# Decode attention: output weights of a group loaded in three transfers of unequal row counts instead of one, and bias sums issued earlier

## Chip, cores, metric

One core of a Trainium2 chip (trn2). The metric is device time of one execution in microseconds (us), taken on the chip. A run counts as slow here when it is over 1.5% above the fastest run of the same kernel. The profile is one execution recorded by the hardware profiler.

PE is the matrix engine, DVE the vector engine, SP the engine that issues the large loads here. SBUF is the on-chip memory of 128 partitions into which the loads write. The profile counts 16 DMA engines. A load comes in packets, and each K and V load here has 16 landings: a landing is taken as the moment at which one engine reports its share of a load done.

## The reference, cut to what matters

One token attends to a cache of 65,536 keys and values, with 16 query heads on 8 key/value heads of 256 numbers; a small MLP and a gate are mixed in.

```python
q = (x @ wq) as 16 heads
scores = q . k / 16        # k: 8 heads x 65536 x 256, bf16
o = softmax(scores) . v    # v: the same size
a = o @ wo                 # wo: 4096 x 448
out = g * a + (1 - g) * b  # b: the MLP; g: one sigmoid of the token
```

K and V are 537 MB together. `wo` is 3.7 MB, eight groups of 512 rows. The time is that of reading K and V: the queue of the large loads, 544.22 MB, is busy for 99.7% of it.

## The kernel before

The K and V cache comes in 48 steps of five or six blocks, each step one transfer of K and one of V over all 128 partitions (40,960 or 49,152 B a partition; only the last V comes in four pieces). SP issues all large loads on one queue. Two K buffers and one V buffer keep the queue full. DVE transposes K, PE makes scores and sums.

The output weights of groups 0 to 6 were one transfer each, behind V loads in the same queue:

```python
def load_wo(g):
    if g >= 1:
        sp.wait_ge(s_oo, g)                       # the last group's weights are used
    sp.dma_start(
        out=wo[:].rearrange("p r c n -> p r (c n)"),            # 128 partitions, 2 x 1792 B each
        in_=A_wo[g * 512:(g + 1) * 512, :].rearrange("(r p c) n -> p r (c n)", r=2, c=2),
    ).then_inc(s_wo, 16)
...
take(dve, s_wo, 16)                               # before the heads of that group are used
```

The end of the program, cut:

```python
pe.wait_ge(s_last[1], 16); upright(edges[1], edges[2])   # V . p, second piece of the last V block
drain_pv(False)                                          # DVE
row = acc + bias                                         # DVE
o_turn(2)                                                # PE, head turn (L685)
pe.wait_ge(s_last[2], 16); turned(edges[2], edges[3])    # PE, turned V blocks (L751)
pe.wait_ge(s_last[3], 16); turned(edges[3], edges[4])
heads()                                                  # DVE, oT (L550)
pe.wait_ge(s_fd, 2)
for a in range(4): matmul(acc4, one_f, row)              # PE, bias sums (L789)
for k in range(4): ... matmul(acc4, oT, wo)              # PE, output matmuls (L799), wait for s_wl[r]
```

The softmax here doesn't subtract the row's maximum and nothing guards it: scores larger than these inputs give would overflow.

## Time and profile before

| | before |
|---|---|
| time, median of 3 | 1265.88 us (1265.81 to 1265.99) |
| bytes read | 544.22 MB, 431 GB/s over the span |
| DMA queue of the large loads | 99.7% of the 16 engines' time |
| PE, DVE busy | 57%, 53% |
| 40,960 B packet, 49,152 B packet | 1514 ns, 1815 ns (8047 of 8064 and 4086 of 4096 packets) |
| 1792 B packet (output weights) | 74 ns (2039 of 2048 packets) |

The first fence is the page's slice view of the kernel before: the span in 40 equal slices, in the DMA line the busy share in tenths, in the next line the rate; then the packets, and the line of the one large queue.

```profile
DMA  9999999999999999999999999999999999999998
GB/s 407 425 435 429 442 435 424 439 433 432 440 430 426 436 434 437 440 426 434 438 427 438 430 436 436 430 432 436 430 443 429 429 439 434 429 442 430 430 436 348
DMA packets 16840, 544.30 MB, mean 431 GB/s; under 512 B 1856, under 2 KB 3906, under 8 KB 4162
...
q1 hardware_dynamic: 16744, 544.22, 99.7%
```

The rate lies at 424 to 443 GB/s between the start and the last slice. The kernel is bound by this stream.

The next fence is the view of stretches, 232 to 248 us, in which the output weights of group 1 come in (columns: stretch, its length, busy time of each engine, granted PE clock, DMA busy share, GB/s).

```profile
232.00:248.00 16.00, 9.17 (x77) 3.52 (x74) 5.91 (x4) 1.33 (x3) 1.69 (x2) 1.00 1.01 435
```

The last one is the chain of work that ended last (start us, duration us, what).

```profile
...
1228.07 30.50 DMA kbuf<-in_A_v_cache_dram
1258.57 0.05 issue
1258.62 1.44 PE misc L751 x48
1260.06 0.48 PE acc L789 x8
1260.54 0.50 PE acc L799 x16
1261.04 0.02 issue
1261.06 0.27 DVE res L806
```

It goes through the third piece of the last V block, then the turned blocks, the bias sums, the output matmuls. The trace's landings (one for each DMA engine of a transfer) show that 15 engines have this piece by 1257.75 us and one by 1258.57 us. The same spread, 1.7 us from first to last with one engine 0.8 us behind the fifteenth, stands in nearly every K and V load (93 of 95 lie between 1.6 and 1.85 us).

### The profile page before, as it was taken

What the parts mean: (1) busy time and instruction counts of PE and PEld (TensorE: products, weight loads), DVE (VectorE), ACT (ScalarE), POOL (GpSimd) and SP (SyncE); (2) the same over time, 40 slices, a digit from 0 to 9 for tenths busy, and PEclk for the clock granted to TensorE, in tenths of its full rate; (3) what the DMA queues carried; (4) which work ended last, traced back from release to release, by engine and by line L of the source; (5) the groups of instructions that cost most, each with busy time, mean ns of one, the idle gap of its engine ahead of it and who ended that gap; (6) DMA issues with size and microseconds to landing.
All of it is one profiled execution on the core that took longest, in us unless ns stands there. A gap on an engine that the chain in (4) does not pass through costs nothing. (4 is left out here: it accounts for less than half of the span.)

```text
span 1264.1 us, 10623 instructions
## 1 busy us (share of the span) xinstructions
PE 722.2 (57%) x4296; PEld 276.3 (22%) x4296; DVE 675.3 (53%) x462; ACT 50.1 (4%) x127; POOL 78.5 (6%) x111
## 2 busy tenths in 40 slices
PE   3855656456554665556654564555645656466556
PEld 1311222122221222112221221222212222122212
DVE  5745554465544555455555555464545645465544
ACT  0000000000000000000000000000000000000000
POOL 1001010110110101101011011000000000000000
PEclk9887777878787787777878787777877778778887
DMA  9999999999999999999999999999999999999998
GB/s 407 425 435 429 442 435 424 439 433 432 440 430 426 436 434 437 440 426 434 438 427 438 430 436 436 430 432 436 430 443 429 429 439 434 429 442 430 430 436 348
DMA packets 16840, 544.30 MB, mean 431 GB/s; under 512 B 1856, under 2 KB 3906, under 8 KB 4162
## 3 DMA queue, kind: packets, MB, share of 16 engines
q1 hardware_dynamic: 16744, 544.22, 99.7%
q8 instruction: 2, 0.03, 0.0%
q10 hardware_dynamic: 90, 0.01, 0.0%
q14 instruction: 4, 0.03, 0.0%
HBM read 544.22 MB, written 0.00 MB: 431 GB/s over the span
## 5 line engine op out<-in xcount | busy, mean ns | idle before, releaser
L661 PE MATMUL sc<-kT,qw 128*128 128x512 bf16 x2048 | 573.5, 438 | 482.9 <-PEq L657 482.9
L532 DVE STREAM_TRANSPOSE kT<-kbuf 128x2048 f32<-128x2048 f32 x256 | 572.8, 2285 | 330.1 <-DVEq L524 330.1
L661 PEld LDWEIGHTS sc<-kT,qw 128*128 128x128 bf16 x2048 | 211.1, 108 | 845.1 <-issue 692.8
L675 PE MATMUL pv<-vbuf,pT 128*4 128x512 bf16 x2008 | 121.2, 390 | 28.8 <-PEq L705 28.7
L543 DVE TENSOR_TENSOR og<-pv,og 128x512 f32<-128x512 f32 x40 | 27.7, 692 | 98.5 <-DVEq L524 97.9
L608 ACT ACTIVATE p_t<-sc 128x512 bf16<-128x512 f32 x48 | 28.7, 597 | 1191.9 <-PE sc L661 1191.9
L675 PEld LDWEIGHTS pv<-vbuf,pT 128*4 128x4 bf16 x2008 | 47.1, 88 | 99.3 <-issue 53.8
L589 DVE STREAM_TRANSPOSE pT<-p_t 128x512 bf16<-128x512 bf16 x32 | 22.8, 712 | 74.1 <-DVEq L524 74.1
L635 POOL TENSOR_SCALAR t_b<-t_b 128x448 f32<-128x448 f32 x14 | 7.9, 564 | 359.1 <-ACT t_b L617 359.1
L639 POOL TENSOR_SCALAR t_b<-t_b,hw 128x448 f32<-128x448 f32 x14 | 8.9, 638 | 334.0 <-ACT t_b L625 334.0
L579 DVE STREAM_TRANSPOSE pT<-p_t 128x512 bf16<-128x512 bf16 x8 | 5.7, 712 | 26.9 <-DVEq L524 26.9
L720 PE MATMUL acc<-wo,oT 128*1 128x448 bf16 x28 | 10.1, 504 | 12.7 <-PEq L717 12.7
L644 POOL TENSOR_TENSOR ymix<-ymix,t_b 128x448 f32<-128x448 f32 x14 | 16.1, 1148 | 1.1
L638 POOL TENSOR_TENSOR t_b<-t_b,u_b 128x448 f32<-128x448 f32 x14 | 15.8, 1127 | 1.2
L643 POOL TENSOR_TENSOR t_b<-t_b,u_b 128x448 f32<-128x448 f32 x14 | 15.8, 1126 | 1.2
L542 DVE COPY og<-pv 128x512 f32<-128x512 f32 x8 | 5.5, 692 | 18.9 <-DVEq L524 18.9
L594 DVE STREAM_TRANSPOSE pT<-p_t 128x512 bf16<-128x512 bf16 x8 | 5.7, 712 | 14.9 <-DVEq L524 14.9
L617 ACT ACTIVATE t_b<-h_bc,b1T,w1T 128x448 f32<-128x448 f32 x14 | 10.5, 748 | 0.0
L631 POOL TENSOR_SCALAR u_b<-h_bc,w1T,b1T 128x448 f32<-128x448 f32 x14 | 10.0, 715 | 4.1 <-DVE hw L428 2.7
L608 ACT ACTIVATION_READ_ACCUMULATOR p_t<-sc 128x1 f32 x48 | 9.3, 194 | 0.0
L685 PEld LDWEIGHTS misc<-mask,og 128*128 128x128 f32 x64 | 8.7, 196 | 2.4 <-DVE og L543 1.3
L477 DVE TENSOR_TENSOR qw<-qr,block 128x32 bf16<-128x32 f32 (+1 forms) x18 | 8.6, 561 | 0.1
(86 smaller groups left out, 77.4 us busy)
## 6 DMA issues: line engine op xcount, KB each, us to landing
kbuf<-in_A_k_cache_dram SPq DMA_DIRECT2D x32, 5120.0 KB, 33.2
vbuf<-in_A_v_cache_dram SPq DMA_DIRECT2D x31, 5120.0 KB, 20.4
kbuf<-in_A_k_cache_dram SPq DMA_DIRECT2D x16, 6144.0 KB, 35.7
vbuf<-in_A_v_cache_dram SPq DMA_DIRECT2D x16, 6144.0 KB, 23.5
wo<-in_A_wo_dram SPq DMA_DIRECT2D x7, 448.0 KB, 23.6
vbuf<-in_A_wq_dram SPq DMA_DIRECT2D x1, 3072.0 KB, 10.3
kbuf<-in_A_v_cache_dram SPq DMA_DIRECT2D x1, 2560.0 KB, 26.0
kbuf<-in_A_v_cache_dram SPq DMA_DIRECT2D x1, 1280.0 KB, 30.5
```

The costliest lines, as they stand in the source:

```text
L532: dve.transpose(out=kT[b][:].bitcast(FP32), in_=kn[:, s * SB * 128:(s + 1) * SB * 128]).then_inc(s_kt, 1)
L543: return dve.tensor_tensor(out=og[:], in0=pv[:], in1=og[:], op=ALU.add)
L589: dve.transpose(out=pT[:], in_=p_t[:]).then_inc(s_pt, 1)
L608: ins = act.activation(out=p_t[:], in_=sc[:], func=ACT.Exp, scale=scale, accum_out=den[:, c:c + 1])
L617: ins = act.activation(out=t_b[:], in_=h_bc[:], func=ACT.Square, scale=w1T[:, b:b + 1], bias=b1T[:, b:b + 1],)
L631: lambda: pool.tensor_scalar(out=u_b[:], in0=h_bc[:], scalar1=w1T[:, b:b + 1], scalar2=b1T[:, b:b + 1], op0=ALU.mult, op1=ALU.add,),
L638: lambda: pool.tensor_tensor(out=t_b[:], in0=t_b[:], in1=u_b[:], op=ALU.mult),
L643: lambda: pool.tensor_tensor(out=t_b[:], in0=t_b[:], in1=u_b[:], op=ALU.mult),
L644: lambda: pool.tensor_tensor(out=ymix[:], in0=ymix[:], in1=t_b[:], op=ALU.add),
L661: ins = pe.matmul(sc[:], lhsT=qw[:, q, at:at + 128], rhs=kv[:, :, q // 2, :, q % 2], start=(first and q == 0), stop=(last and q == 7), ski ...
L675: ins = pe.matmul(pv[32 * a:32 * a + 4, :], lhsT=pT[:, k, :, ROW0 + s], rhs=vt[:, j * DH:(j + 2) * DH], start=first and k < 4, stop=last a ...
L720: ins = pe.matmul(acc[0:1, 0:D], lhsT=oT[:, k:k + 1], rhs=wo[:, r, cc, :], start=False, stop=False, skip_group_check=True,)
```

## The change

The intent, as far as the diff shows it: give some DMA engines more rows of the output weights and others fewer, so that the engines finish together (the author's reading), and take the bias sums out of the end.

```diff
+SHARES = (
+    (96, 16, 16), (112, 11, 5), (112, 9, 7), (112, 13, 3), (112, 10, 6), (112, 12, 4), (112, 14, 2),
+)
@@
-            sp.dma_start(
-                out=wo[:].rearrange("p r c n -> p r (c n)"),
-                in_=A_wo[g * 512:(g + 1) * 512, :].rearrange("(r p c) n -> p r (c n)", r=2, c=2),
-            ).then_inc(s_wo, 16)
+            rows = A_wo[g * 512:(g + 1) * 512, :].rearrange("(r p c) n -> p r (c n)", r=2, c=2)
+            lo = 0
+            for n in SHARES[g]:
+                sp.dma_start(
+                    out=wo[lo:lo + n].rearrange("p r c n -> p r (c n)"), in_=rows[lo:lo + n]
+                ).then_inc(s_wo, 16)
+                lo += n
@@
-                        take(dve, s_wo, 16)
+                        take(dve, s_wo, 48)
@@
         o_turn(2)
+        pe.wait_ge(s_fd, 2)
+        for a in range(4):
+            pe.matmul(... one_f, row ...)          # bias sums, cut
         pe.wait_ge(s_last[2], 16)
         turned(edges[2], edges[3])
         ...
-        pe.wait_ge(s_fd, 2)
-        for a in range(4):
-            pe.matmul(... one_f, row ...)          # bias sums, cut
```

On how many engines a transfer of few rows runs, the traces show in counts, if each landing is one engine's. The three 14-row loads of before have 14 landings each. The seven loads of output weights have 16 each in before; in after they have 48 in group 0 (96, 16 and 16 rows) and 32 in each of groups 1 to 6, as 16 + 11 + 5, 16 + 9 + 7 and so on come to. So in groups 1 to 6 an engine carries a row of both small transfers, of one or of none; with the 112 rows shared equally, seven each, it gets at most one row more or less than eight. That is an estimate from the counts.

More of the change, by code (lines that the diff above doesn't have):

```diff
@@ L780, in critical @@
         o_turn(2)
+        pe.wait_ge(s_fd, 2)
+        for a in range(4):
+            pe.matmul(
+                acc4[32 * a:32 * a + 1, 0:DQ], lhsT=one_f[:, 0:1], rhs=row[:, DQ * a:DQ * (a + 1)],
+                start=True, stop=False, tile_position=(0, 32 * a), skip_group_check=True,
+            )
         pe.wait_ge(s_last[2], 16)
@@ L786, in critical @@
         heads().then_inc(s_fd, 1)
-        pe.wait_ge(s_fd, 2)
-        for a in range(4):
-            pe.matmul(
-                acc4[32 * a:32 * a + 1, 0:DQ], lhsT=one_f[:, 0:1], rhs=row[:, DQ * a:DQ * (a + 1)],
-                start=True, stop=False, tile_position=(0, 32 * a), skip_group_check=True,
-            )
         pe.wait_ge(s_fd, 3)
```

## The prediction

> **What bounds the kernel.** The DMA engines, from start to end. The page's slice table gives DMA 9 tenths or more in 39 of 40 slices, the queue table 99.7% busy on the one large queue, 544.22 MB at 431 GB/s. The records of single DMA packets are the same all through: 40960 B take 1514 ns, 49152 B take 1815 ns, with no gap on any engine from about 12 us to 1250 us. An engine that has fallen behind stays behind. In every large transfer the 16 landings keep the same spread, 1.7 us from first to last. Fifteen engines lie within 0.93 us, one lags 0.8 us behind the fifteenth. That laggard arises at 29.5 us, when a 16 KB instruction fetch sits on it (1109 ns, and the next packet takes 2315 ns).
>
> The chain of waits ends with this laggard: the third piece of the last V block lands at 1258.57 us (its other 15 engines are done by 1257.75), then PE L751 1.44 us, the bias matmuls L789, the output matmuls L799.
>
> **What the change does.** [...] the 14-row loads have 14 data packets each. [...] A row is two 1792 B packets spaced 71 ns, so 0.142 us: at most +0.85 us or -0.85 us on an engine at the end. Bytes stay the same. Added: 14 issues on SP's queue (about 0.45 us each, hidden, as loads are queued 20 to 35 us ahead) and some 6 to 14 semaphore packets per engine, about 6 ns each: 0.04 to 0.08 us.
>
> The bias matmuls (0.55 us for the group) now run after the head turn that ends at 1258.07, in PE's idle 0.54 us before L751. Afterwards L799 can start when the heads are ready (about 1260.30 instead of 1260.46): 0.15 us, if the last output weights (landing at 1260.0 and 1260.41) let it.
>
> **How much is critical.** [...] its 0.8 us lead is mostly removed and the whole tail moves up, until the next limit: a second 16 KB instruction fetch at 1257.98 us makes another engine end within 0.05 us of the laggard, so the last weights may bind instead. Gain 0.3 to 0.9 us. [...] it gets slower still: loss up to 0.8 us. [...] I take the change's author to have aimed at it, 2 to 1.
>
> **Prediction.** 1265.3 us (0.05% faster), 8 in 10 between 1264.6 and 1266.6. Faster by over 2%: 0.00; within 2%: 1.00; slower: 0.00.
>
> **What would show it.** Landings of a K or V load should narrow from 1.7 us in steps of up to 0.14 us per group from group 1 on; the third V piece should land before 1258.57; the bias matmuls should stand before L751 and L799 should follow the heads directly; the large-packet times should not change.
>
> **What would make it wrong.** [...] small transfers opening gaps on some engines; the last weights or the second fetch taking back the gain.

The gain of 0.3 to 0.9 us stood for the case that the lagging engine gets fewer rows than before, the loss of up to 0.8 us for the case that it gets more, weighed 2 to 1; 0.15 us was foretold for the bias sums. The sum came to 1265.3 us, 0.6 us under the 1265.88 us of before. The 0.85 us is six rows of 0.142 us, one in each of groups 1 to 6 (the estimate above). The "6 to 14" semaphore packets of an engine are the author's guess: the trace has 128 more, eight an engine in the mean, and in before the next packet mostly starts 6 ns after one (1558 of 1764), so 0.05 us.

## The result and the profile after

| | before | after |
|---|---|---|
| time, median of 4 runs each | 1265.85 us | 1280.67 us (1279.56 to 1280.89) |
| ratio of the fast runs | | 1.0115, 95% interval 1.0098 to 1.0133 |
| mean rate | 431 GB/s | 426 GB/s |
| spread of the 16 landings, a V load near the end | 1.7 us | 3.9 us |

A ratio is the mean time of one kernel's fast runs over that of the other's in the same rounds, so it is not quite the ratio of the two medians. The kernel got 14.8 us slower, 1.2%. That is within 2%, but far outside the stated range.

The slice view of the kernel after:

```profile
DMA  9999999999999999999999999999999999999997
GB/s 410 408 428 432 438 435 435 414 434 432 431 435 411 437 438 432 435 406 431 438 430 435 403 436 437 435 429 408 436 432 433 435 405 433 438 431 433 432 436 324
DMA packets 16968, 544.30 MB, mean 426 GB/s; under 512 B 1984, under 2 KB 4034, under 8 KB 4290
...
q1 hardware_dynamic: 16872, 544.22, 99.6%
```

The busy share is as full as before and the bytes are the same. But the rate has seven dips, to 403 to 414 GB/s: slices 2, 8, 13, 18, 23, 28 and 33 (408 414 411 406 403 408 405), one for each load of output weights in groups 0 to 6. Only 128 more packets stand in the count, all of 4 B (semaphore increments). The view of stretches shows the same for group 1:

```profile
232.00:248.00 16.00, 11.60 (x83) 4.40 (x81) 6.81 (x4) 0.67 (x3) 0.00 (x0) 0.93 0.98 382
```

382 instead of 435 GB/s, with the DMA still 0.98 busy. At 16 us that is 0.85 MB less, 1.95 us of the stream at 435 GB/s. So a DMA that counts as busy here (0.98 and 1.01 of this stretch) may be moving 382 or 435 GB/s.

The packet records say which packets grew. The next fence sums, for each load of output weights and the 14 us after it, what the packets took beyond their usual 74, 1514 and 1815 ns, as a mean of the 16 engines ("all sizes" has the 49,152 B packets and a little of the 4 B ones too). It is worked out from the records, not an answer of the profile.

```
group of the load        0     1     2     3     4     5     6    sum
before, all sizes, us  0.00  0.00  0.00  0.00  0.00  0.00  0.00   0.0
after, all sizes, us   1.59  1.39  1.62  1.88  1.98  1.95  1.93  12.3
  of it 1792 B packets 0.64  0.55  0.62  0.70  0.68  0.61  0.55   4.4
  of it 40960 B        0.85  0.76  0.89  1.04  1.11  1.11  1.15   6.9
mean 1792 B packet, ns  114   108   113   118   117   112   109    (before: 74)
```

So the weights' own packets took half as long again, and the K packets behind them lost more still. The engines' landings confirm the sum: the 46th V load lands, as a mean of the 16 engines, 11.75 us later than before (1233.41 against 1221.66 us), and its last engine another 1.65 us later, as the last engine is now 2.81 us behind the mean instead of 1.16 us. Together 13.4 us of the 13.7 us by which the profiled spans differ.

The chain at the end:

```profile
...
1241.80 31.49 DMA kbuf<-in_A_v_cache_dram
1273.29 0.05 issue
1273.34 0.40 PE misc L759 x8
1273.73 0.02 issue
1273.76 0.17 DVE oT L558
1273.93 0.04 issue
1273.97 0.74 PE acc L807 x15
1274.71 0.02 issue
1274.74 0.27 DVE res L814
```

The bias sums are gone from the chain, as foretold, but the chain now hangs on a last V piece that lands late. The output matmuls L807 take 0.74 us instead of 0.50 us, as the second half of them waits for the last output weights, which land at 1274.28 us:

```profile
1274.33 0.10 PEld L807 LDWEIGHTS acc<-wo,oT 128*1 128x1 bf16 x8 [0.25 <-DMA wo<-in_A_wo_dram]
```

### The profile page after: what moved, and what is told of

It reads as the page before. It is cut to its first block, busy times and chain, and to the rows that moved or that the text cites. A ratio compares the mean times of both kernels' runs of the same rounds, so it can differ in the third digit from the quotient of the medians.

```text
span 1277.7 us, 10637 instructions
## 1 busy us (share of the span) xinstructions
PE 723.3 (57%) x4296; PEld 276.6 (22%) x4296; DVE 675.3 (53%) x462; ACT 50.1 (4%) x127; POOL 78.5 (6%) x111
## 3 DMA queue, kind: packets, MB, share of 16 engines
q1 hardware_dynamic: 16872, 544.22, 99.6%
HBM read 544.22 MB, written 0.00 MB: 426 GB/s over the span
## 5 line engine op out<-in xcount | busy, mean ns | idle before, releaser
L683 PE MATMUL pv<-vbuf,pT 128*4 128x512 bf16 x2008 | 123.9, 397 | 37.1 <-PEq L713 36.8
L728 PE MATMUL acc<-wo,oT 128*1 128x448 bf16 x28 | 8.6, 443 | 12.7 <-PEq L725 12.7
L460 PE MATMUL sc<-vbuf,xw 128*128 128x512 bf16 x32 | 10.0, 490 | 0.0
## 6 DMA issues: line engine op xcount, KB each, us to landing
kbuf<-in_A_v_cache_dram SPq DMA_DIRECT2D x1, 1280.0 KB, 30.7
```

What stands on the lines that cost most here:

```text
L460: last = e.matmul(q_ps[:], lhsT=xw[:, k, HKV - 1 - n:HKV - 1 - n + 128], rhs=rhs, start=(n == 0 and k == 0), stop=(n == HKV - 1 and k >= K ...
L683: ins = pe.matmul(pv[32 * a:32 * a + 4, :], lhsT=pT[:, k, :, ROW0 + s], rhs=vt[:, j * DH:(j + 2) * DH], start=first and k < 4, stop=last a ...
```

## Experiments

**Theory.** The partitions that a transfer writes decide what it costs: a transfer over all 128 partitions costs the time of its bytes, one over 112, 96, 64, 16 or 11 of them can hold up itself and the K loads behind it. In before the K loads, all over 128 partitions, run at 40,960 B in 1510 ns from start to start, 27.1 GB/s an engine. The mechanism that the author assumed behind this is shown by no trace or run here; it is left out, and cut from the expectations below.

**Rivals.** The number of transfers, with their semaphore packets and issues. Transfers on fewer than 16 engines, or unequal engines. The HBM side of the smaller transfers. The order on PE.

### Parts of the change (e1, e4, e11)

e1 is the change without the split loads: `load_wo` and `take(dve, s_wo, 16)` as before, the bias sums moved.

> Kernel before, with only the bias matmuls moved ahead of the turned V blocks (one whole 128-row load of the output weights, as before). Theory (the split loads alone cost the time): about 1265.7 us, 0.1 to 0.2 us under before, since the four output matmuls can start when the heads are ready. Rival (the reordering on PE costs the time): near 1280 us.

Measured 1265.85 us (5 runs), before 1265.83 us in the same rounds; ratio 1.000, interval 0.9986 to 1.0014. The split loads are the whole loss; the foretold gain of 0.1 to 0.2 us is not there either. PE's lines at the end, before and in e1 (timeline, PE alone: start us, length, line, in brackets the idle time just before and its releaser):

```profile
1256.97 1.10 PE L685 MATMUL misc<-mask,og 128*128 128x2 f32 x8 [0.80 <-DVE og L543]
1258.62 1.44 PE L751 MATMUL misc<-pT,kbuf 128*128 128x2 bf16 x48 [0.54 <-DMA kbuf<-in_A_v_cache_dram]
1259.99 0.55 PE L789 MATMUL acc<-row,one_f 1*1 1x112 f32 x8
1260.46 0.54 PE L799 MATMUL acc<-wo,oT 128*1 128x112 bf16 x16
```

```profile
1257.11 1.40 PE L685 MATMUL misc<-mask,og 128*128 128x2 f32 x8 [0.80 <-DVE og L543]
1258.44 0.55 PE L783 MATMUL acc<-row,one_f 1*1 1x112 f32 x8
1258.92 1.44 PE L751 MATMUL misc<-pT,kbuf 128*128 128x2 bf16 x48
1260.62 0.54 PE L799 MATMUL acc<-wo,oT 128*1 128x112 bf16 x16 [0.25 <-DVE oT L550]
```

The idle time of 0.54 us ahead of L751 was just as long as the bias sums need. In this profile the head turn began 0.14 us later and took 1.40 us instead of 1.10 us, so the bias sums ended after the V piece had landed (1258.73 us by the landings) and pushed L751 from 1258.62 to 1258.92 us. What was saved behind the turned blocks was paid ahead of them.

e4 is the other part alone: the split loads, the bias sums where they were.

```diff
 (kernel before)
-  one transfer of 128 rows, take 16
+  for n in SHARES[g]: three transfers, take 48
```

> Kernel before, with only the split loads of the output weights, the bias matmuls where they were. Theory: the whole loss, 1280 to 1281 us. Rival (PE order): near 1266 us.

One fast run of 1280.47 us and one slow of 1316.53 us. The fast one gives the whole loss.

> The kernel with only the split loads once more, as its first submission had one fast and one slow run. Theory: fast runs at 1280 to 1281 us, the whole loss of the change. Rival (part of the loss comes from the PE order): under 1278 us.

Four runs: 1303.08 us, and 1341.95, 1323.78 and 1328.05 us, which count as slow. That is against both expectations; none of the runs is at 1280 us. The run of 1303.08 us is 1.8% above e4's fast run, the same kernel on another chip, so beside e4 it would count as slow too. Its profile shows what was added:

```profile
GB/s 404 402 381 392 388 381 396 380 410 431 434 439 408 429 434 435 435 405 432 437 432 431 408 430 437 436 430 404 432 435 435 436 402 433 439 432 429 432 438 328
```

From the load of group 0 to about 264 us the rate stays at 380 to 410 GB/s, then it is normal again outside the dips. In that stretch the packet records give 1698 or 1700 ns for the 40,960 B packets of all 16 engines (instead of 1514 ns), though only whole 128-row K and V loads run there. Some 1750 large packets, from 60 to 259 us, are longer by 12%, about 22 us on each engine, and the span is 22.5 us longer than that of e4's profile. The rhythm sets in with the split load of group 0 (54.7 us) and is gone after that of group 1 (260.5 to 265.2 us). So a split load can leave the whole stream in a slower, steady rhythm that lasts long after it, and here it ended with the next one. No profile of before shows this, and none of the 28 runs of before beside the experiments left the stretch of 1265.45 to 1266.25 us. In the fast runs of the split kernels the packets are back to 1514 ns some 5 to 8 us after each load begins, and the four runs of the changed kernel show nothing of it (1279.56 to 1280.89 us). What the rhythm consists of, and why a load starts or ends it, is open. That the slow runs are longer stretches of it is a guess: none of them was profiled.

### The number of transfers (e2)

```diff
-  one transfer of 128 rows
+  for r, lo, hi in ((0, 0, 2), (1, 0, 1), (1, 1, 2)):     # three transfers, each of 128 rows
+      sp.dma_start(out=wo[:, r, lo:hi, :]..., in_=rows[:, r, lo:hi, :]...).then_inc(s_wo, 16)
-  take(dve, s_wo, 16)
+  take(dve, s_wo, 48)
```

> Kernel before, with the output weights of every group loaded by three transfers that each span all 128 rows and a part of the columns (1792, 896 and 896 B a row). The number of transfers is that of the changed kernel (21 in all), the packets are more (24 instead of 16 per engine and group). Theory [...]: within 1 us of before, 1266 to 1267 us. Rival (more and smaller transfers, more semaphore packets, more issues on SP): near 1280 us.

1266.23 us (4 runs), ratio 1.0003. The stretch of group 1:

```profile
232.00:248.00 16.00, 9.26 (x77) 3.59 (x75) 5.91 (x4) 1.33 (x3) 1.69 (x2) 1.00 1.03 438
```

Three transfers, half as many packets again, as many semaphores and issues as in the changed kernel: 438 GB/s. Its 1792 B packets took 74 ns as a mean, as in before. The number of transfers is innocent; cutting columns is free here (1266.23 against 1265.83 us), cutting rows is not (1280.67 us).

### Fewer engines, or unequal engines (e3, e12)

e3 cuts the rows in two equal halves, 64 and 64, and e12 in 112 and 16. All row counts are multiples of 16. For 16, 96 and 112 rows the trace of after has 16 landings a transfer (48 for the three of group 0, 32 for 112 + 11 + 5); that 64 rows run on 16 engines too, and that every engine then carries eight rows a group, is an estimate from these counts.

```diff
-SHARES = ((96, 16, 16), (112, 11, 5), ...)
+SHARES = ((64, 64),) * 7          # e3, take 32
+SHARES = ((112, 16),) * 7         # e12, take 32
 (bias sums as in before)
```

> Kernel before, with the output weights of every group loaded by two transfers of 64 rows each, both on all 16 engines, no engine gets more rows than another. [...] 7 groups times 0.7 to 1.2 us, so 1271 to 1274 us. Rival (the transfers on fewer than 16 engines cost the time, or the imbalance of rows does): 1266 us. Rival (number of transfers): two instead of three, so some 1270 to 1276 us, not told apart by this run.

> Kernel before, with the output weights of every group loaded as 112 and 16 rows: the first of the changed kernel's transfers as it is, the 16 rows in one transfer on all 16 engines, so every engine has 8 rows and none more than another. Theory [...]: about the loss of the changed kernel, 1278 to 1282 us. Rival (transfers on fewer than 16 engines, or unequal engines, cost the time): about 1266 us.

e3: 1284.57 us (1283.41 and 1285.74), ratio 1.0148. e12: 1279.89, 1277.81 and 1278.71 us, and one slow run of 1388.32 us; ratio of the fast runs 1.0097. So, by that estimate, the loss is there with no engine favoured and none left out: 12.7 us over before in e12, 1.8 us for each group. It was there in the change too, in group 0, whose 96, 16 and 16 rows have 16 landings each: 1.59 us. Two halves are worse than three parts: 18.7 us over before, 2.7 us for each group. (The stretch of group 1 in e3, which begins 2 us later there.)

```profile
234.00:250.00 16.00, 10.50 (x76) 3.76 (x74) 5.20 (x3) 0.29 (x1) 0.00 (x0) 0.89 0.99 368
```

The foretold size missed: 0.7 to 1.2 us a group against 2.7 us. A whole load of a group takes 1.1 us (16 packets an engine, 71 ns apart), so the loss is more than twice the load itself. The spread of the landings of a V load also grew without any imbalance of rows, from 1.7 us to 4.8 us in e3. e12, with equal rows too by the estimate, has 3.6 us, the change 3.9 us. So nearly all of the wider spread after the change needs no moved rows.

### Where the bytes land, and nothing else (e5, e6, e7)

Three kernels put one extra transfer of 128 KB behind each of the 32 K loads of five blocks, into a part of the K buffer that is not read. All give right results. They differ in the destination; e6 and e7 read the very same 16 source rows.

```diff
 def load_k(i):
     ... the K load ...
+    if steps[i] == 5:
+        sp.dma_start(out=kbuf[i % 2][ROWS, at:at + W], in_=kv_src(A_k_cache, i)[0:N, 0:W])...
+    # e5: ROWS = all 128, 1024 B each    e6: ROWS = 0:106:7, 8192 B each    e7: ROWS = 112:128, 8192 B each
```

> Kernel before, plus one extra transfer of 128 KB behind each of 30 to 32 K loads of five blocks, into a part of the K buffer that nobody reads (results stay right): 128 rows of 1024 B, so 8192 B per engine[...]. Both theories: bytes alone, 8192 B at the traced 27 GB/s per engine is 0.30 us, with eight packets some 0.33 us, so about 10 us more: 1276 us.

> The same extra 128 KB behind the same K loads, as 16 rows of 8192 B, one per engine, written to partitions 0, 7, 14 ... 105. [...] 0.6 to 0.9 us per transfer, so 1285 to 1295 us, clearly under the run with rows 112 to 127. Rivals (a transfer of few rows is slow by itself; reading few HBM rows is slow): the same time as the run with rows 112 to 127, within 3 us.

> The same extra 128 KB behind the same K loads, from the same source rows, as 16 rows of 8192 B, one per engine, written to partitions 112 to 127. [...] at least 1.2 us per transfer: 1303 us or more. Rivals: the same time as the run with partitions 0, 7, 14 ..., within 3 us.

### Chosen partitions against mere closeness (e9, e10)

The same with 8 rows of 8192 B, read from the same source rows: `ROWS = 0:32:4` in e9, `ROWS = 0:128:16` in e10.

> Kernel before, plus an extra 64 KB behind the same 32 K loads: 8 rows of 8192 B, one on each of 8 engines, written to partitions 0, 4, 8 ... 28. [...] 0.30 us per transfer at most, 1276 us, and all 8192 B packets near 309 ns. Rival (partitions close together are slow): clearly slower than the run with partitions 0, 16, 32 ...

> The same 64 KB from the same source rows, 8 rows of 8192 B on 8 engines, written to partitions 0, 16, 32 ... 112, as far apart as they can be. [...] at least 0.6 us per transfer, 1285 to 1297 us, slower than the run with partitions 0, 4, 8 ... Rival (only partitions close together are slow, or only the count of rows matters): no slower than that run.

The five together. The last column is the time over before of the same rounds, divided by 32.

| run | extra rows, partitions | time, us | per transfer, us |
|---|---|---|---|
| e5 | 128 x 1024 B, all | 1276.94 | 0.35 |
| e9 | 8 x 8192 B, 0, 4, ... 28 | 1275.51 | 0.30 |
| e6 | 16 x 8192 B, 0, 7, ... 105 | 1300.27 | 1.08 |
| e10 | 8 x 8192 B, 0, 16, ... 112 | 1294.36 | 0.89 |
| e7 | 16 x 8192 B, 112 to 127 | 1323.15 | 1.79 |

In e5 and e9 the extra transfer costs its bytes, 0.30 to 0.35 us, with 8 rows as with 128 (8192 B at 27.1 GB/s are 0.30 us; the 8192 B packets of e9 took 310 ns as a mean, against 407 ns in e7). In e10, e6 and e7 it costs three to six times that, 0.89 to 1.79 us, with the same bytes per engine (an estimate: 128 KB over 16 engines, 64 KB over 8) and, in e9 and e10 as in e6 and e7, the same source rows. So neither the HBM side nor the smallness of the transfers tells e9 from e10. And e9 against e10 rules out that close partitions are slow as such: eight partitions within the first 32 are free, eight partitions spread over all 128 are not. e9 and e10 differ in nothing but the partitions written, and so do e6 and e7 (1.08 and 1.79 us). What makes one set of partitions free and another not, the five runs do not show; nor do they show why 16 rows (e6) cost more than 8 (e10).

Where it was not free, at least 0.6 us in e10, 0.6 to 0.9 us in e6 and at least 1.2 us in e7 were expected; 0.89, 1.08 and 1.79 us were measured. So the two bounds hold, far exceeded, and e6 lies above its range. In e7 the large K and V packets before 1200 us are longer by 30.7 us on each engine, in sum, in e6 by 16.8 us, in e10 by 15.4 us and in e9 by 2.0 us. So about half of the time lost in e7, e6 and e10 (57.4, 34.5 and 28.6 us) falls on the loads around the extra transfer. How a transfer slows the loads around it is open.

### A version that might beat both (e8)

The kernel before, with the row for the bias made earlier on DVE, and the bias sums ahead of the head turn instead of behind it.

```diff
         rden_gate(den_ps[:, 0:2])
+        row = acc + bias                       # DVE, moved up from behind drain_pv
         pe.wait_ge(s_last[1], 16); upright(edges[1], edges[2])
         drain_pv(False)
+        bias sums                              # PE, moved up
         o_turn(2)
```

> Kernel before, with one whole load per group, the bias row made on DVE before the last drain, and the bias matmuls ahead of the head turn, in PE's idle time before that turn (0.8 us in the trace of before; the matmuls take 0.5 us). Theory (ahead of the turned blocks they only filled time that was no longer free, as the head turn ended later): the head turn and the turned blocks start as in before and the output matmuls right behind the heads: 1265.6 to 1265.75 us, 0.1 to 0.2 us under before; too small for the interval, to be read from the trace. Rival (the end is bound by the landing of the last output weights): no change.

1265.83 us (5 runs) against 1265.80 us, ratio 1.0001. PE's lines at the end of e8:

```profile
1257.17 0.37 PE L781 MATMUL acc<-row,one_f 1*1 1x112 f32 x8 [0.84 <-DVE row L772]
1257.77 1.10 PE L685 MATMUL misc<-mask,og 128*128 128x2 f32 x8 [0.23 <-DVE og L543]
1258.79 1.41 PE L751 MATMUL misc<-pT,kbuf 128*128 128x2 bf16 x48
1260.46 0.55 PE L799 MATMUL acc<-wo,oT 128*1 128x112 bf16 x16 [0.26 <-DVE oT L550]
```

The output matmuls do follow the heads. But in this profile the last K block's scores ended 0.66 us later than in the profile of before, as PE took longer for the block before it, so the chain at the end ran through DVE and PE and not through the V pieces. Two chains end within some tenths of a microsecond of each other here; shortening one by 0.15 us is not seen. No version that beats before was found.

## Why the prediction was wrong

- **"What bounds the kernel": right.** The stream at 431 GB/s bounds it, and the kernel lost nearly what the stream lost: 11.75 us in the engines' mean and 1.65 us in the spread, of a 13.7 us longer span.
- **"A row is two 1792 B packets spaced 71 ns, so 0.142 us: at most +0.85 us or -0.85 us on an engine at the end": this is the step that failed.** It priced a row as time on the engine that carries it, as if it didn't matter to which partitions that engine writes. In the changed kernel a 1792 B packet took 108 to 118 ns as a mean, and the packets of the next loads grew more. The missing term was 1.4 to 2.0 us for each of seven loads (12.3 us in the sum of packet times), where the prediction's whole sum was under 1 us. e12 shows it (1.8 us a load) with rows that are equal on all engines by the estimate, e2 shows it gone with whole columns (ratio 1.0003), e9 and e10 show that the partitions written can decide (0.30 and 0.89 us). That the partitions are what decides in the split loads too is argued from these runs; how they do is not shown. The prediction did not ask what a destination of 112 rows does.
- **"Bytes stay the same": right, and no help.** The same 544.22 MB went at 426 instead of 431 GB/s.
- **"Landings of a K or V load should narrow": wrong.** They went from 1.7 us to 3.9 us. e3, with equal rows, widens them to 4.8 us.
- **"The large-packet times should not change": wrong**, and this was the profile's plainest sign: 6.9 of the 12.3 us are in the 40,960 B packets.
- **"14 issues on SP's queue, hidden" and the semaphore packets: right.** e2 has the same number and costs 0.4 us in the medians (1266.23 against 1265.83 us), which is inside the interval.
- **Which way the lagging engine's rows change: not settled, and not what decided.** In e9, which gives eight engines an extra row each, the landings part in two groups of eight, and in one V load (the 21st) a single engine stands 0.84 us behind the rest of the group without extra rows, as the laggard stands in before. That speaks for a laggard that the 8-row transfer leaves out. But in the 41st load that distance is only 0.37 us, the landings carry no engine numbers, and no trace shows whether the small transfers of the change leave out the same engines.
- **"Afterwards L799 can start when the heads are ready: 0.15 us": the step is there, the gain is not.** The chain after runs from the heads straight to the output matmuls, but e1 alone gained nothing, since the idle time that the bias sums were put into was exactly full. The danger that the prediction named, the last weights, came true as well: in the changed kernel they hold up the second half of L807 by 0.25 us.
- **"Within 2%": right** (1.0115), but by luck: the cost that it left out happened to be 1.2%. The range of 1264.6 to 1266.6 us was far too narrow. It allowed for the sign of a small effect and not for a new cost; "small transfers opening gaps on some engines" was listed as a danger but not given room. There were no gaps either: the large queue is busy for 99.6% of the span, with longer packets.

## What to carry to other kernels

In this stream of whole 128-partition loads, other loads were free where they kept to 128 partitions too: three column pieces cost nothing here (ratio 1.0003), two row halves cost 2.7 us for a load that takes 1.1 us. So if such a load must be cut, try columns first. Before moving rows between DMA engines, write down which partitions the pieces will then write to, and measure what those cost: here eight rows cost 0.30 us on partitions 0, 4, ... 28 and 0.89 us on 0, 16, ... 112. And don't read a DMA busy share near 1.00 as full rate (0.98 stood beside 382 GB/s, 1.01 beside 435): compare GB/s by stretch and the time of packets of one size.
